# Query scores of an agent attention: copied out of PSUM by ScalarE, maximum taken from SBUF, subtraction on GpSimd

## The chip, the cores and the metric

One core of one Trainium2 chip runs the whole program. The metric is the device time of one execution in microseconds (us). PE is TensorE, DVE is VectorE, ACT is ScalarE, POOL is GpSimd, SP is SyncE, which issues the transfers. PEld are PE's weight loads.

## The reference

Four batches (B = 4) of N = 12480 tokens with C = 128 channels and 49 agents, then a feed-forward layer with d_ff = 2048 on all 49920 tokens.

```python
def sm(a, b):
    s = scale * (a @ b.transpose(0, 2, 1))
    s = s - s.max(-1, keepdims=True)
    e = np.exp(s)
    return e / (e.sum(-1, keepdims=True) + 1e-09)
a2k = sm(agents, k)
agent_v = a2k @ v
q2a = sm(q, agents)
x = q2a @ agent_v
h = x @ w_in
out = (h * np.cos(h)) @ w_out
```

What the change touches is the `s - s.max` of `q2a`: for each token, 49 scores against the agents, less their maximum.

## The kernel before

Tokens are taken in groups of 960 (8 tiles of 120 tokens); a batch has 13 groups, the run 52. A group is one unit of query work (its scores, exponentials, weights, and the transposed weights `pT`) and one unit of feed-forward work.

The **main loop** (L545 to L582) has 832 steps, 16 for each group: two chunks of 480 tokens by eight pairs of d_ff blocks. A step multiplies the query weights with the folded matrix `a` into one of three two-bank PSUM buffers `ph` (PE, L553, two matmuls), takes a cosine of it on ACT into `c` (L556), and combines both on DVE into `r` (L558), which frees the `ph` buffer. Four steps later PE multiplies `r` with `w_out` into an accumulator (L575) that ACT copies out after eight steps (L577, `osb`). So `ph` goes round a ring: PE, ACT, DVE, PE, with three buffers.

Everything else is laid between those steps by a hand-written plan (L450 to L541): the query scores and key scores of later groups, the exponentials in a few bursts, the agents' values, and the folding of the next batch's matrix. A **query** (L336) loads 960 tokens, multiplies their eight tiles with the agents into one PSUM bank (L90, 16 PE records), takes the maxima on DVE (L345) and subtracts them on DVE into a slice of the SBUF tile `e` (L352). The bank comes from a pool of two (`small()`), of which the accumulator `po` holds one nearly always; the other serves queries, key scores, transposes and value sums in turn, and the next user's matmuls wait until the last reader is done. Three queries (`wide=True`, before the main loop) use a `ph` buffer instead; 49 use `small()`. The maxima go to `mx2`, a tile with two buffers.

Several queries form a **piece**, and a **burst** takes one exponential of a whole piece (L356), after which DVE sums it (L360) and takes reciprocals. The exponential needs another ACT table than the cosine, so a burst is a table load, the exponentials of the key scores (L216) and of the piece, and a table load back. In each of the batches after the first there are three bursts; at the first of them three queries of a later piece are laid right beside it (`beside`, L482 to L486, L519). Key scores (L156) are copied out of PSUM by ACT (L173) and DVE takes a running maximum of the copy (L184); beside the very first burst of the main loop three of them are copied by DVE instead (`by_vector`, L490).

POOL multiplies `e` with the reciprocals (L366, 10 steps before the group's first step), PE transposes (L375, from 7 steps before it), ACT copies (L377), POOL makes `pT` of it (L380, L381, four instructions). POOL also subtracts the key maxima (L212, three long instructions for a batch) and adds up the key exponentials (L224).

The order on each engine is laid down when the program is built: the framework places an instruction once its inputs are ready by its own estimate of the times, and of those ready the one that comes first in the program. It is pinned to program order only for the exponentials and the first loads (`keep_in_program_order`). An engine then works through its own list, and an instruction that waits holds up those behind it.

Of the kernel before, what the change touches and what calls it, by code (L numbers as in the profile page):

```python
# [9 lines left out]
F32 = mybir.dt.float32  # L10
# [5 lines left out]
AX = mybir.AxisListType  # L16
# [3 lines left out]
TT = 120  # L20
GT = 8
HT = GT // 2
# [18 lines left out]
def agent_attention_cos_ffn(ctx, tc, qT, kT, v, agT, w_in, w_out, outT):  # L41
    nc = tc.nc
    NB, _, N = qT.shape
    NA = agT.shape[2]
# [39 lines left out]
    def scores(sb, src, b, ps):  # L84

        xt = sb.tile([P, GRP], F32, name="xt", bufs=3)
        load(xt, src)
        ps = ps[:TT, :GT * NA].rearrange("p (t a) -> p t a", a=NA)
        for t in range(GT):
            nc.tensor.matmul(ps[:, t, :], xt[:, t * TT:(t + 1) * TT], ag[:, b, :], start=True, stop=True)  # L90
        return ps

    def scores_twice(xt, src, b, ps):

        load(xt, src)
        ps = ps[:TT, :, :HT * 2 * NA].rearrange("p h (t x a) -> p h t x a", x=2, a=NA)
        for t in range(GT):
            nc.tensor.matmul(ps[:, t // HT, t % HT], xt[:, t * TT:(t + 1) * TT], twice(ag[:, b, :]),  # L98
                             start=True, stop=True)
        return ps[:, :, :, 0, :]  # L100
# [201 lines left out]
    with ExitStack() as pools:  # L302
        sb = pools.enter_context(tc.tile_pool(name="sb", bufs=2))
# [3 lines left out]
        def small():  # L307
            return ps_1.tile([P, 512], F32, name="one")

        def pair():  # L310
            return ps_h.tile([P, 2, 512], F32, name="ph")
# [4 lines left out]
        a = [sb.tile([KR, DFF], F32R, name=f"a{i}", bufs=1) for i in range(2)]  # L316
# [16 lines left out]
        e_of, rz_of = {}, {}  # L333
        PIECES = 5

        def query(n, piece, wide=False):  # L336
            b, g = n // NG, n % NG
            src = qT[b, :, g * GRP:(g + 1) * GRP]
            if wide:
                ps = scores_twice(sb.tile([P, GRP], F32, name="xt", bufs=3), src, b, pair())  # L340
            else:
                ps = scores(sb, src, b, small()).rearrange("p (h t) a -> p h t a", h=2)
            mx = sb.tile([TT, GT], F32, name="mx2")
            mx = mx.rearrange("p (h t) -> p h t", h=2)
            nc.vector.reduce_max(mx, ps, axis=AX.X)  # L345
            if n == piece[0]:
                e = sb.tile([TT, PIECES * GT, NA], F32, name="e", bufs=4)
                rz = sb.tile([TT, PIECES * GT], F32, name="rz2", bufs=4)
                for i, k in enumerate(piece):
                    e_of[k], rz_of[k] = e[:, i * GT:(i + 1) * GT], rz[:, i * GT:(i + 1) * GT]  # L350
                    e_of[piece], rz_of[piece] = e[:, :len(piece) * GT], rz[:, :len(piece) * GT]
            nc.vector.tensor_sub(e_of[n].rearrange("p (h t) a -> p h t a", h=2), ps,  # L352
                                 mx.unsqueeze(3).to_broadcast([TT, 2, HT, NA]))

        def query_exp(piece):
            tc.keep_in_program_order(nc.scalar.activation(e_of[piece], e_of[piece], AF.Exp, scale=SC))  # L356
# [53 lines left out]
        for n in first:  # L410
            pre(NG, query, n, first, True)
# [41 lines left out]
        def extra(n, f, *args, dense=False):  # L453


            while n in taken or (n - LAG) % NP not in ((1, 2, 3, 4, 5) if dense else (1, 3, 5)):
                n += 1
            taken.add(n)
            plan(n, f, *args)
            return n  # L460
# [5 lines left out]
        def spread_out(todo, t, end):  # L466

            for i, lot in enumerate(todo):
                t = extra(t, *lot) + 1
                if i + 1 < len(todo):  # L470
                    t += max(0, (end - t) // (len(todo) - i - 1) - 1)
            return t
# [6 lines left out]
        def scored(piece):  # L479
            return [(query, n, piece) for n in piece]  # L480
# [7 lines left out]
        t = spread_out(scored(early), 0, 0) + 2  # L488
# [3 lines left out]
        for b in range(1, NB):  # L492
            o, ps = (b - 1) * PER, pieces[b - 1]
# [7 lines left out]
            t = spread_out(both, t, o + BURSTS[0] - 14)  # L501
            plan(t, ab[b].top)
            t = extra(t, ab[b].across)
            t = extra(t + 1, ab[b].spread)
# [4 lines left out]
            for k, at in enumerate(BURSTS):  # L509
# [7 lines left out]
                t = at + 6  # L517
# [4 lines left out]
                else:  # L522
                    todo = []
                    for g in range(lots[2][0], NG):
                        plan(t, ab[b].add, g)
                        t = extra(t, ab[b].values, g) + 2
                t = spread_out(todo, t, o + BURSTS[min(k + 1, 2)] - 4)
            plan(t, ab[b].total)
            t = extra(t + 1, ab[b].inverse) + 1
            i = b % 2  # L530
            for c in range(DFF // 512):
                t = extra(t, ab[b].project, c, a[i]) + 1
            t = extra(t, ab[b].project_out, wio, b1[i], b2[i])
# [3 lines left out]
        for piece in pieces[NB - 1]:  # L537
            at = (NB - 1) * PER + BURSTS[0]
            t = spread_out(scored(piece), t, at - 6)
# [5 lines left out]
        for n in range(NSTEP + LAG):  # L545
            pinned[0] = n < NP
            if n < NSTEP:
# [6 lines left out]
                h = ph[:, :, :CH]  # L554
# [42 lines left out]
    with tc.If(far):  # L597
        with ExitStack() as pools:
            sb = pools.enter_context(tc.tile_pool(name="gsb", bufs=2))
# [8 lines left out]
            p = sb.tile([TT, HT, 2 * HI], F32, name="p", bufs=1)  # L608
# [114 lines left out]
```

## Time and profile before

| | |
|---|---|
| median of 3 runs | 1256.7 us (1256.64 to 1257.83) |
| the profiled execution's own time | 1252.39 us |
| its span, first to last instruction | 1250.6 us |
| mean granted TensorE clock | 0.986 of full speed |
| busy share of the span | PE 94%, DVE 87%, ACT 77%, POOL 25% |
| share of the chain that ended last | PE 68%, DVE 14%, ACT 11%, issue 4%, DMA 2% |

Busy shares are means over stages. PE's records overlap one another, so its 94% is not 94% of its work. The chain follows the last instruction back, at each step to what released it or to the instruction before it on its engine, so that a wait which nothing else covers shows up in it. Until 120 us the kernel sets up the first batch and starts the main loop; the stages of batches two to four follow, about 300 us each (from 120, 420 and 720 us); after about 960 us only the last batch's own groups are left.

### The profile page before, as it was taken

To read this page: it belongs to the slowest core of one execution; us is meant where nothing else is said; L and a number is where in the kernel's file an instruction comes from. 1 tells how busy PE (TensorE), PEld (TensorE's weight loads), DVE (VectorE), ACT (ScalarE), POOL (GpSimd) and SP (SyncE) were. 2 spreads that over 40 slices of the span, in tenths; PEclk is the share of its full clock that TensorE was granted. 3 is DMA by queue.
4 is the path that set the end of the run, shared out by engine and by line. 5 is a ranking of instruction groups with operands and counts; after the bars stand their busy time and mean duration, and the time that the engine had idled before them with its cause. 6 is when DMAs were issued, how large, how long until landed. Compare 5 with 4: busy or idle time off the path is not lost.

```text
span 1250.6 us, 17276 instructions
## 1 busy us (share of the span) xinstructions
PE 1177.9 (94%) x6349; PEld 957.6 (77%) x6349; DVE 1089.8 (87%) x1220; ACT 959.0 (77%) x1127; POOL 314.1 (25%) x340
## 2 busy tenths in 40 slices
PE   7989999899999999989999999998999999998997
PEld 7877877778887887877787887877778776776674
DVE  5888888878889888887889889887888999999997
ACT  2357777777778777777878777777887888889996
POOL 1301212512321212162332212115331322113220
PEclk9989999999999999989999999998999999999999
DMA  8963232224422232322241232322321001000000
GB/s 307 246 185 111 80 110 68 76 77 127 126 65 79 79 98 77 95 79 83 73 130 50 78 110 65 97 93 79 96 80 48 32 32 48 17 32 17 32 32 35
DMA packets 39190, 107.74 MB, mean 86 GB/s; under 512 B 4345, under 2 KB 4729, under 8 KB 39097
## 3 DMA queue, kind: packets, MB, share of 16 engines
q1 hardware_dynamic: 39096, 106.55, 27.0%
q8 instruction: 52, 0.85, 0.3%
q14 instruction: 42, 0.34, 0.1%
HBM read 80.97 MB, written 25.56 MB: 85 GB/s over the span
## 4 chain that ended last, share of the span: by engine, by line
PE 68%; DVE 14%; ACT 11%; issue 4%; DMA 2%; POOL 0%; SPq 0%; ACTq 0%; DVEq 0%
PE ph L553 25%; PE one L575 18%; PE one L90 12%; DVE r L558 11%; ACT c L556 6%; PE one L235 5%; ACT osb L577 3%; PE one L375 2%; PE ph L98 2%; PE one L571 2%; PE one L572 2%; DVE mx L345 1%; DMA raw<-w_out 1%; DMA xt<-kT 1%; PE one L266 1%
## 5 line engine op out<-in xcount | busy, mean ns | idle before, releaser
L558 DVE SCALAR_TENSOR_TENSOR r<-c,ph 128x960 fp32r<-128x960 f32 x832 | 924.9, 1149 | 91.1 <-ACT c L556 83.1
L556 ACT ACTIVATE c<-ph 128x960 f32<-128x960 f32 x832 | 794.2, 977 | 220.5 <-PE ph L553 200.9
L553 PE MATMUL ph<-pT,a 113*128 113x480 f32 x1664 | 544.2, 408 | 26.7 <-DVE r L558 24.3
L575 PE MATMUL one<-r,w 128*128 128x480 f32 x1664 | 518.2, 391 | 3.9 <-ACT osb L577 3.5
L553 PEld LDWEIGHTS ph<-pT,a 113*128 113x128 f32 x1664 | 285.7, 191 | 138.8 <-DVE r L558 63.5
L575 PEld LDWEIGHTS one<-r,w 128*128 128x128 f32 x1664 | 311.1, 191 | 52.4 <-ACT osb L577 6.9
L90 PEld LDWEIGHTS one<-ag,xt 128*120 128x120 f32 x1408 | 175.5, 189 | 42.7 <-ACT osb L577 24.4
L366 POOL TENSOR_TENSOR p<-e,rz 120x392 f32<-120x392 f32 x52 | 47.5, 917 | 574.2 <-PE one L375 468.5
L90 PE MATMUL one<-ag,xt 128*120 128x49 f32 x1408 | 174.8, 268 | 16.8 <-issue 8.6
L381 POOL TENSOR_TENSOR pT<-p,pT 49x480 fp32r<-49x480 f32 x104 | 126.1, 1212 | 8.0
L380 POOL CAST pT<-p 49x480 fp32r<-49x480 f32 x104 | 60.5, 582 | 153.0 <-ACT p L377 149.9
L235 PEld LDWEIGHTS one<-s,vt 120*128 120x128 f32 x624 | 77.3, 191 | 10.0 <-DVE av L240 3.6
L235 PE MATMUL one<-s,vt 120*128 120x98 f32 x624 | 79.0, 273 | 2.5 <-DVE av L240 1.4
L577 ACT COPY osb<-one 128x480 f32<-128x480 f32 x104 | 57.7, 554 | 2.9 <-PE one L575 2.9
L224 POOL TENSOR_TENSOR es<-es,s 120x392 f32<-120x392 f32 x36 | 36.7, 1019 | 59.1 <-ACT s L216 56.7
L345 DVE TENSOR_REDUCE mx<-one 120x8 f32<-120x392 f32 x49 | 27.5, 561 | 17.8 <-PE one L90 17.8
L212 POOL TENSOR_TENSOR s<-s,mxb 120x1568 f32<-120x1568 f32 (+1 forms) x9 | 31.6, 3544 | 44.8 <-DVE mxb L208 44.8
L571 PE MATMUL one<-pT,b 113*128 113x480 f32 x104 | 40.2, 387 | 0.0
L572 PE MATMUL one<-pT,b 113*128 113x480 f32 x104 | 40.1, 385 | 0.0
L375 PEld LDWEIGHTS one<-ident,p 120*113 120x113 f32 x208 | 29.2, 177 | 13.6 <-ACT osb L577 9.1
L375 PE MATMUL one<-ident,p 120*113 120x120 f32 x208 | 34.1, 275 | 2.7 <-ACT osb L577 2.7
L377 ACT COPY p<-one 113x480 f32<-113x480 f32 x52 | 29.0, 558 | 6.4 <-PE one L375 5.9
(91 smaller groups left out, 503.2 us busy)
## 6 DMA issues: line engine op xcount, KB each, us to landing
xt<-qT SPq DMA_DIRECT2D x52, 480.0 KB, 3.5
vt<-v SPq DMA_DIRECT2D x104, 240.0 KB, 3.4
outT<-osb SPq DMA_DIRECT2D x51, 480.0 KB, 2.6
xt<-kT SPq DMA_DIRECT2D x46, 480.0 KB, 3.5
c<-kT SPq DMA_DIRECT2D x6, 480.0 KB, 5.7
raw<-w_in SPq DMA_DIRECT2D x8, 256.0 KB, 5.1
raw<-w_out SPq DMA_DIRECT2D x8, 256.0 KB, 6.6
outT<-osb SPq DMA_DIRECT2D x2, 240.0 KB, 2.8
```

The lines of the kernel that those rows point to most:

```text
L90: nc.tensor.matmul(ps[:, t, :], xt[:, t * TT:(t + 1) * TT], ag[:, b, :], start=True, stop=True)
L235: nc.tensor.matmul(po, vt[:, t, :], twice(e[:, t, :]), start=(t == 0 and (g == 0 or not lone)), stop=(t == GT - 1 and (g == NG - 1 or not ...
L375: nc.tensor.transpose(pt[:KR, t * TT:(t + 1) * TT], p_in[n % 2][:, t, :KR], ident[:TT, :TT])
L380: nc.gpsimd.tensor_copy(pT[own, c], p[own])
L381: nc.gpsimd.tensor_sub(pT[other, c], p[own], pT[own, c].bitcast(F32))
L553: nc.tensor.matmul(ph[:, j, :CH], ai[:, f], pTs[q % 3][:, c], start=True, stop=True)
L556: nc.scalar.activation(cos, h, AF.Sin, bias=HALF_PI, scale=1.0)
L558: nc.vector.scalar_tensor_tensor(r, cos, 1.0, h, op0=ALU.subtract, op1=ALU.mult)
L571: nc.tensor.matmul(po, b1[k], pTs[q % 3][:, c], start=False, stop=False)
L572: nc.tensor.matmul(po, b2[k], pTs[q % 3][:, c], start=False, stop=False)
L575: nc.tensor.matmul(po, w1[:, f, :], r[:, j, :], start=(f == 0), stop=(f == NF - 1))
L577: nc.scalar.copy(osb[:, c * CH:(c + 1) * CH], po)
```

## The change

The 49 queries on `small()` are changed. ACT copies the scores from the PSUM bank into their slice of `e`; DVE takes the maxima from `e` in SBUF; POOL subtracts them in place in `e`. The three wide queries keep both operations on DVE and on PSUM. The tiles `e` and `rz2` are now allocated ahead of `mx2`. Nothing is pinned, and no transfer, matmul or exponential is added or moved.

```diff
             else:
                 ps = scores(sb, src, b, small()).rearrange("p (h t) a -> p h t a", h=2)
-            mx = sb.tile([TT, GT], F32, name="mx2")
-            mx = mx.rearrange("p (h t) -> p h t", h=2)
-            nc.vector.reduce_max(mx, ps, axis=AX.X)
             if n == piece[0]:
                 e = sb.tile([TT, PIECES * GT, NA], F32, name="e", bufs=4)
...
-            nc.vector.tensor_sub(e_of[n].rearrange("p (h t) a -> p h t a", h=2), ps,
-                                 mx.unsqueeze(3).to_broadcast([TT, 2, HT, NA]))
+            e = e_of[n].rearrange("p (h t) a -> p h t a", h=2)
+            if not wide:
+                nc.scalar.copy(e, ps)
+                ps = e
+            mx = sb.tile([TT, GT], F32, name="mx2")
+            mx = mx.rearrange("p (h t) -> p h t", h=2)
+            nc.vector.reduce_max(mx, ps, axis=AX.X)
+            on = nc.vector if wide else nc.gpsimd
+            on.tensor_sub(e, ps, mx.unsqueeze(3).to_broadcast([TT, 2, HT, NA]))
```

## Rows read from the trace of the kernel before

**Rows 1.** The chain that ended last, whole run, share of the span by line

```profile
by line: PE ph L553 24.9%; PE one L575 17.9%; PE one L90 11.9%; DVE r L558 10.9%; ACT c L556 6.0%; PE one L235 5.0%; issue 3.9%; ACT osb L577 3.3%; PE one L375 1.8%; PE ph L98 1.7%; PE one L571 1.7%; PE one L572 1.6%; DVE mx L345 1.3%; DMA 
```

**Rows 2.** The same chain in a steady stretch, 420 to 480 us

```profile
by line: PE ph L553 27.3%; PE one L90 23.2%; PE one L575 19.1%; DVE r L558 11.1%; ACT osb L577 5.6%; ACT c L556 4.9%; DVE mx L345 2.4%; PE one L375 2.1%; PE one L571 1.9%; PE one L572 1.8%; issue 1.0%
```

**Rows 3.** Busy time, 420 to 480 us: PE, PEld, DVE, ACT, POOL; then line 173 alone

```profile
420.00:480.00 60.00, 57.38 (x324) 47.57 (x323) 53.00 (x55) 46.61 (x58) 13.11 (x15) 1.00 0.27 84
...
420.00:480.00 60.00, 2.42 (x5) 1.00 0.27 84
```

**Rows 4.** Chain pieces around one steady query: start us, us, what

```profile
447.28 1.16 DVE r L558
448.43 0.47 DVE mx L345
448.91 1.07 DVE r L558
...
450.02 0.70 PE ph L553 x2
```

**Rows 5.** Timeline of the same query: start us, us, engine, line, [idle before it <-releaser]

```profile
446.27 2.73 ACT L556 ACTIVATE c<-ph 128x960 f32<-128x960 f32 x3 [1.18 <-PE ph L553]
...
450.02 0.70 PE L553 MATMUL ph<-pT,a 113*128 113x480 f32 x2 [0.33 <-DVE r L558]
...
450.36 5.61 DVE L558 SCALAR_TENSOR_TENSOR r<-c,ph 128x960 fp32r<-128x960 f32 x5
```

**Rows 6.** Waits of the whole run: us in total, times, longest us

```profile
DVE mx L345 <- PE one L90: 17.8, 12, 2.7
...
PE one L90 <- issue: 8.6, 3, 2.9
```

**Rows 7.** Timeline of one of five queries that follow each other closely

```profile
300.49 0.57 DVE L345 TENSOR_REDUCE mx<-one 120x8 f32<-120x392 f32 x1 [1.10 <-PE one L90]
...
301.42 0.97 ACT L556 ACTIVATE c<-ph 128x960 f32<-128x960 f32 x1 [1.81 <-PE ph L553]
...
302.26 0.67 PE L553 MATMUL ph<-pT,a 113*128 113x480 f32 x2 [0.22 <-DVE r L558]
```

**Rows 8.** Timeline of the first burst with queries beside it

```profile
241.04 1.49 ACT L356 ACTIVATE e<-e 120x1568 f32<-120x1568 f32 x1
...
243.84 2.70 ACT L556 ACTIVATE c<-ph 128x960 f32<-128x960 f32 x3
...
245.46 0.56 DVE L352 TENSOR_TENSOR e<-one,mx 120x392 f32<-120x392 f32 x1
...
246.12 2.82 PE L90 MATMUL one<-ag,xt 128*120 128x49 f32 x16 [2.87 <-issue]
```

**Rows 9.** Busy time right after it (engines as in Rows 3), granted TensorE clock 0.56

```profile
246.00:253.00 7.00, 6.88 (x27) 6.21 (x28) 6.31 (x10) 2.48 (x3) 4.93 (x6) 0.56 0.27 78
```

**Rows 10.** Groups by line and shape: times, busy us, mean ns, idle before, releaser

```profile
L352 DVE TENSOR_TENSOR e<-one,mx 120x392 f32<-120x392 f32 x49 | 27.4, 560 | 0.2
...
L173 ACT COPY s<-one 120x392 f32<-120x392 f32 x36 | 17.4, 484 | 5.7 <-PE one L90 5.4
...
L360 DVE TENSOR_REDUCE rz<-e 120x8 f32<-120x392 f32 x1 | 0.6, 551 | 0.0
```

**Rows 11.** A subtraction as a piece of the chain

```profile
835.14 0.48 DVE e L352
```

**Rows 12.** GpSimd's multiplication of the same shape: ns minimum, median, maximum

```profile
L366 POOL TENSOR_TENSOR p<-e,rz x52: 838/846/3740, 45.9 to 1176.3; 120x392 f32<-120x392 f32 x52
```

**Rows 13.** Shortest way from a last subtraction to the piece's exponential

```profile
109.75 0.56 DVE L352 TENSOR_TENSOR e<-one,mx 120x392 f32<-120x392 f32 x1
...
112.98 1.85 ACT L356 ACTIVATE e<-e 120x1960 f32<-120x1960 f32 x1
```

**Rows 14.** A long stretch of GpSimd reading SBUF, and DVE beside it

```profile
231.27 5.59 DVE L558 SCALAR_TENSOR_TENSOR r<-c,ph 128x960 fp32r<-128x960 f32 x5
...
231.49 10.53 POOL L212 TENSOR_TENSOR s<-s,mxb 120x1568 f32<-120x1568 f32 x3 [14.80 <-DVE mxb L208]
```

## The prediction, made before the changed kernel was run

> **What bounds the kernel now.** I read the chain that ended last first, whole and then in a steady stretch. PE's four main lines hold most of it, and what PE waits for shows as DVE r 10.9%, ACT c 6.0%, ACT osb 3.3% and DVE mx 1.3% [rows 1]. 1.3% of 1250.6 us is 16.3 us: that is what the maxima (L345) cost on the path. In the steady stretch mx has 2.4% of 60 us, three pieces of 0.48, one for each query there, and the list adds up to 100%, so neither the key scores' copy on ACT (L173) nor their running maximum on DVE (L184) is on the chain there, though five copies ran [rows 2, 3]. Then the busy times of that stretch: DVE 53.0 of 60 us (88%), ACT 46.6 (78%), POOL 13.1 (22%) [rows 3]. PE's 57.4 overstates it: a pair of L553 that takes 0.70 after a wait stands at some 0.44 in the chain where pairs follow each other. So DVE is the engine with least to spare, and the loss is latency: PE waits for a `ph` buffer that r frees late.
>
> How a query makes r late is in its own rows. In the steady case mx stands between two r's; the second ends 0.48 later, and PE, which has already sat 0.33 us, starts the next pair right on its end [rows 4, 5]. In the close case mx heads DVE's list before its scores exist: DVE sits 1.10 us, the r behind it has had its input all along (ACT idle for 1.81), and PE waits 0.22 for that r [rows 7]. DVE waited for scores like this twelve times, 17.8 us in all [rows 6]. Three of these, of 2.7 us, stand in bursts; nine of about 1.08 are close cases (17.8 - 8.1 = 9.7).
>
> **The change, part by part.** The sum goes against the profiled execution, 1252.4 us with 1250.6 of span; the median of the runs is 1256.7, 4.3 above it, and I add the same 4.3 at the end.
>
> *The subtraction leaves DVE:* 49 x 0.560 = 27.4 us of work [rows 10]. On the chain it shows only five times, 0.48 to 0.54 each (one of them: [rows 11]), so 2.4 us. Ends: 0, and all 27.4 if every r behind a subtraction is on the path. I take 2.4, since the chain is the nearer row; after the steady subtraction five r's do run back to back, but PE has other work there [rows 5].
>
> *The maximum stays on DVE.* Reading SBUF it costs what it did: 0.551 us for the same shape [rows 10]. But it now comes after a copy, so its place changes. In the nine close cases it can no longer stand ahead of an r that is ready; PE gets back its 0.22 us and the slow restart after it, 0.67 against 0.44 for a pair: 0.45 x 9 = 4.0. Ends: 0, and 9 x 1.1 = 9.9 if all of DVE's wait comes back. In the steady cases the chain has 16.3 less twelve pieces of 0.57 = 9.5 us, about twenty pieces. Either mx still falls between two r's (0) or it falls ahead of or behind the pair that matters (9.5). The row does not decide: it is the framework's order. I take half, 4.7.
>
> *The copy on ACT:* 49 x 0.484 = 23.7 us, from the key scores' copy of the same shape [rows 10]. What hides it is ACT's idle time while PE works through the scores, 1.18 us in the steady case and 1.81 in the close one [rows 5, 7]. Without that cover each copy puts the c behind it, and its r, 0.4 to 0.48 us late. Lower end 0: the key copies are absent from the steady chain [rows 2]. Upper end: as often as the accumulator's copy, 3.3% or 41 us for 104 copies [rows 1], 0.40 each, 19.5 for 49. The key copy is the same shape and place, so near the lower end: I take a tenth of the upper, 2.0 lost.
>
> *The subtraction on POOL:* nearest the multiplication of the same shape with the same kind of broadcast, 0.846 [rows 12]; ends 0.838 and 3.74, its slowest. In all 49 x 0.85 = 41 us on an engine 25% busy. Cover: nothing needs the result until the piece's exponential. A query takes copy 0.48 + max 0.55 + subtraction 0.85 = 1.9 us instead of 1.1, and the shortest way from the end of a last subtraction to its exponential is 112.98 - 110.31 = 2.7 us [rows 13], so the 0.8 fits. If POOL is behind one of its long instructions (10.5 us for three [rows 14]) the exponential waits, and ACT's cosines behind it. These come ahead of the first burst of a batch, whose own piece was finished before; I take 0, at most one such instruction, 3.5 us, for three batches. There is a new wait on DVE too: `mx2` has two buffers, which POOL now frees, so the third of three quick queries waits for POOL with r's behind it. That can happen only at the same three bursts; 0 to 2.4 us each, taken as 0.
>
> *The PSUM bank* is freed by the copy, not by the subtraction. It matters at those three bursts: PE's third block of scores waits until DVE's subtraction at 245.46 ends, 2.87 us [rows 8], three times 8.6 us in all [rows 6]. After the wait the granted clock is 0.56 for 7 us [rows 9], near the lower of the two levels (1.2 of 2.4 GHz); 7 x 0.44 = 3.1 us more. So a burst holds about 6 us that hang on when a bank comes free, 18 us in all. With the change ACT must free it, and ACT has the exponentials until 242.53, a table load, and three cosines from 243.84 to 246.54 [rows 8]. A copy just before those cosines frees the bank 1.7 us sooner, one behind them 1.0 us later. I take 0 and keep both ends as rivals.
>
> No transfer is added; SP's loads wait for the same matmuls as before. The three wide queries keep their operations.
>
> **Sum:** 2.4 + 4.0 + 4.7 - 2.0 = 9.1 us gained; 1252.4 - 9.1 = 1243.3, and with the 4.3 **1247.6 us**.
>
> **A rule weighed against the trace.** While POOL ran 10.5 us of subtractions that read SBUF, five r's beside them took 5.59 us [rows 14]; without POOL, 5.61 [rows 5]. r is not slowed. The Trainium skill, "Perfetto Trace Analysis", section "Optimizing Scalar/DVE Operations", says that offloading to GPSIMD may make sense if DVE is saturated, but that the two share an SBUF read port, so that moving work between them might not help. For r the trace does not bear the second half out. By the rule, each subtraction would hold up one r by its own 0.85 us, and I keep it as the last rival.
>
> **The rivals.**
> *Bursts close too.* The copies fall before the cosines at the three bursts, the 2.87 us gaps shrink by 1.7 and the clock stays up: 3 x (1.7 + 3.1) = 14.4 beyond the forecast, **1233 us**. For it: the gap's end is a DVE instruction queued behind a 1.8 us sum, and the copy needs neither. Against: ACT is full there.
> *No difference.* mx keeps its place between the r's and only the subtraction's 2.4 us come back, or the steady gain is eaten in the bursts: **1254 to 1258 us**. For it: the same rule of order as before places mx.
> *Slower.* At the three bursts ACT's list has both exponentials ahead of the first query's copy. Its bank comes free at 243.0 instead of 240.6, so the second block of scores starts about 1.5 us late; its copy stands behind the three cosines, so the third block starts at about 247.5 instead of 246.1; with the clock low for a further 2 us that is 1.5 + 1.4 + 0.9 = 3.8 a burst, 11.4 in all. If mx also keeps its place, only the 2.4 come back: +9, **1266 us**. It decides as soon as a copy stands behind both the exponentials and the cosines. For it: exponentials are pinned ahead, and key copies beside the very first burst were given to DVE. Against: PE has idle time there anyway.
> *The shared port.* 49 x 0.85 = 41 us if every subtraction stalls an r on the path: up to 1247.6 + 41 = **1289 us**. Against it: the row above.
>
> **How the numbers follow.** Forecast 0.42, bursts close too 0.18, no difference 0.17, slower 0.19, port 0.04. A measurement tells about 0.2% (2.5 us) from no change. Forecast (1241 to 1254) and bursts lie on the faster side; of "no difference" 0.03 is faster, 0.12 same, 0.02 slower; the last two are slower: faster 0.63, same 0.12, slower 0.25. The range goes from 1232, just below the centre of the lowest rival (a third of it left out, 0.06), to 1265, about the centre of the slower one (half left out, 0.09), and leaves out the port: 0.19. The forecast alone has 1241 to 1254: the steady term at 9.5 or 0, the copy at 0 or 4.
>
> **What would show it.** Right: DVE about 27 us less busy, ACT 24 and POOL some 41 more; mx nearly gone as something that waits for PE; mx on the chain at most half of 16 us; no copy of scores among the large lines of the chain. The subtraction on POOL at 0.85. At 238 to 253 us PE's gap about as long as before, with the clock falling after it. Wrong: copies between PE and c on the chain, c waiting behind a copy that itself waits for PE; DVE's maximum waiting for POOL; a longer gap in the three bursts, or none; r longer than 1.15 us beside POOL.

## The result and the profile after

The changed kernel took 1242.4 us (median of four runs, 1237.0 to 1246.1) against 1256.7 for the kernel before: a ratio of 0.989 with an interval of 0.985 to 0.993. Run again (an experiment below) it took 1239.1 against 1256.6, ratio 0.990 (0.987 to 0.993). So 1247.6 was 5 us too slow, inside the range; the gain was 14 to 17 us where the sum had 9.1. The profiled execution was 1242.7 us with 1241.0 of span; that of the second time was 1237.0 with 1235.2.

The changed kernel's page begins with the span and each engine's busy time, share and instructions:

```profile
span 1241.0 us, 17334 instructions
...
PE 1180.0 (95%) x6349; PEld 975.0 (79%) x6349; DVE 1067.3 (86%) x1171; ACT 982.4 (79%) x1176; POOL 353.5 (28%) x389
```

Before, DVE had 1089.8, ACT 959.0 and POOL 314.1: work has moved as the diff says. The changed kernel's groups by line and shape, which answer to [rows 10] (line numbers have shifted by 4; the copy is L351, the maximum L355, the subtraction L357), show what each instruction costs:

```profile
L562 DVE SCALAR_TENSOR_TENSOR r<-c,ph 128x960 fp32r<-128x960 f32 x832 | 924.1, 1149 | 96.2 <-ACT c L560 90.4
...
L357 POOL TENSOR_TENSOR e<-e,mx 120x392 f32<-120x392 f32 x49 | 41.3, 844 | 155.7 <-DVE mx L355 150.9 <-ACT osb L581 3.5
L355 DVE TENSOR_REDUCE mx<-e 120x8 f32<-120x392 f32 x49 | 27.2, 555 | 8.2 <-ACT e L351 8.2
L351 ACT COPY e<-one 120x392 f32<-120x392 f32 x49 | 23.8, 487 | 18.7 <-PE one L90 18.4
```

The prices are those of the sum: 0.844 against 0.85, 0.555 against 0.551, 0.487 against 0.484. r has 1149 ns, as before.

The waits of the whole run (us in total, times, longest) say where DVE mattered less. First the changed kernel, then the one before:

```profile
PE ph L557 <- DVE r L562: 14.2, 39, 4.3
...
PE one L90 <- ACT e L351: 10.9, 3, 3.6
...
DVE mx L355 <- ACT e L351: 8.2, 7, 1.7
```

```profile
PE ph L553 <- DVE r L558: 24.3, 74, 4.3
```

TensorE waited for r 39 times and not 74, 10 us less. In place of the three waits for DVE's subtraction [rows 6] there are three for ACT's copy, a little longer, and at another block of scores (see the bursts below). Nothing on DVE waits for POOL. In the chain of the whole run the maxima (mx) have 10.5 us where they had 16.6; "at most half" was named as a sign of being right, and it did not come.

The steady stretch, 411 to 471 us, has the same shape as [rows 2, 4]. The chain by line, some of its pieces, and the timeline of the same query:

```profile
by line: PE ph L557 27.8%; PE one L90 24.2%; PE one L579 21.4%; DVE r L562 11.1%; ACT c L560 4.9%; ACT osb L581 4.7%; DVE mx L355 2.4%; PE one L576 1.8%; PE one L575 1.8%; issue 0.8%
...
425.14 1.15 DVE r L562
426.29 0.47 DVE mx L355
426.76 1.07 DVE r L562
...
427.88 0.70 PE ph L557 x2
```

```profile
423.19 0.49 ACT L351 COPY e<-one 120x392 f32<-120x392 f32 x1 [0.23 <-PE one L90]
...
424.38 0.47 PE L379 MATMUL one<-ident,p 120*113 120x120 f32 x3
...
426.21 0.55 DVE L355 TENSOR_REDUCE mx<-e 120x8 f32<-120x392 f32 x1
...
426.68 5.42 DVE L562 SCALAR_TENSOR_TENSOR r<-c,ph 128x960 fp32r<-128x960 f32 x5
...
428.11 0.85 POOL L357 TENSOR_TENSOR e<-e,mx 120x392 f32<-120x392 f32 x1
```

Before, the transposes for the next weights, which use the same bank, came only after the subtraction:

```profile
450.78 0.57 PE L375 MATMUL one<-ident,p 120*113 120x120 f32 x4
```

The maximum still stands between two r's with its 2.4%, and TensorE still takes its next pair behind the second r. But the copy lets the transposes (424.38) start ahead of the maximum, where they stood behind the subtraction, and the stretch got shorter. Where, the copy-outs of the output rows (osb) tell: there are 104 at fixed places in the work, and the differences of their start times cut a run into stretches that can be laid beside each other. **Start** is up to the 1st; **first burst** from the 1st to the 5th; **three bursts** the sum of 13th to 15th, 39th to 41st and 65th to 67th; **rest** all else up to the 103rd; **four steady** queries lie between the 27th and the 35th, **two close** ones between the 35th and the 39th (both are part of the rest). All in us, one profiled run each:

| run | start | first burst | three bursts | rest | four steady | two close |
|---|---|---|---|---|---|---|
| before | 97.3 | 48.9 | 91.9 | 998.3 | 89.10 | 46.27 |
| changed | 95.5 | 54.1 | 94.3 | 982.7 | 87.44 | 44.55 |
| changed, again | 91.0 | 51.5 | 94.8 | 983.4 | 87.44 | 44.57 |
| subtraction on VectorE | 92.3 | 48.0 | 96.0 | 992.6 | 88.99 | 45.00 |
| copy on VectorE | 102.9 | 51.0 | 86.5 | 991.3 | 88.35 | 45.35 |
| only beside the bursts | 97.8 | 51.3 | 97.0 | 999.1 | 89.07 | 46.29 |
| beside old | 92.7 | 53.0 | 91.3 | 981.9 | 87.45 | 44.56 |
| beside by VectorE | 97.1 | 54.0 | 85.4 | 982.1 | 87.44 | 44.56 |
| first burst later | 93.1 | 50.7 | 94.5 | 983.3 | 87.44 | 44.56 |
| beside and 3 to 7 by VectorE, later | 103.4 | 50.8 | 84.8 | 982.8 | 87.44 | 44.57 |
| beside by VectorE, later | 91.3 | 49.2 | 84.4 | 982.8 | 87.45 | 44.55 |
| query 3 old | 104.8 | 52.7 | 94.7 | 983.5 | 87.44 | 44.57 |
| no maximum, no subtraction | 95.8 | 52.7 | 97.6 | 971.6 | 86.13 | 43.91 |
| no subtraction | 97.1 | 53.1 | 93.4 | 983.0 | 87.44 | 44.56 |

The change gains some 15 us in the rest, 0.41 for a steady query and 0.86 for a close one, and gives back 2.4 to 2.9 in the three bursts and 2.6 to 5.2 in the first. The start varies from run to run for a reason that was not found (last section), and also holds a gain, found below.

### The profile page after: what moved, and what is told of

It reads as the page before. It is cut to its first block, busy times and chain, and to the rows that moved or that the text cites. A ratio compares the mean times of both kernels' runs of the same rounds, so it can differ in the third digit from the quotient of the medians.

```text
span 1241.0 us, 17334 instructions
## 1 busy us (share of the span) xinstructions
PE 1180.0 (95%) x6349; PEld 975.0 (79%) x6349; DVE 1067.3 (86%) x1171; ACT 982.4 (79%) x1176; POOL 353.5 (28%) x389
## 3 DMA queue, kind: packets, MB, share of 16 engines
q1 hardware_dynamic: 39096, 106.55, 27.4%
## 4 chain that ended last, share of the span: by engine, by line
PE 70%; DVE 12%; ACT 12%; issue 4%; DMA 0%; POOL 0%; ACTq 0%; SPq 0%; DVEq 0%
PE ph L557 25%; PE one L579 18%; PE one L90 12%; DVE r L562 9%; ACT c L560 6%; PE one L235 5%; ACT osb L581 3%; PE ph L235 3%; PE one L575 2%; PE one L576 2%; PE one L379 1%; PE ph L98 1%; ACT e L360 1%; DVE mx L355 1%; PE one L266 1%
## 5 line engine op out<-in xcount | busy, mean ns | idle before, releaser
L562 DVE SCALAR_TENSOR_TENSOR r<-c,ph 128x960 fp32r<-128x960 f32 x832 | 924.1, 1149 | 96.2 <-ACT c L560 90.4
L90 PEld LDWEIGHTS one<-ag,xt 128*120 128x120 f32 x1408 | 180.6, 194 | 49.5 <-ACT osb L581 27.9
L90 PE MATMUL one<-ag,xt 128*120 128x49 f32 x1408 | 180.2, 273 | 21.5 <-ACT e L351 10.9
L370 POOL TENSOR_TENSOR p<-e,rz 120x392 f32<-120x392 f32 x52 | 44.3, 857 | 474.2 <-PE one L379 397.2
L357 POOL TENSOR_TENSOR e<-e,mx 120x392 f32<-120x392 f32 x49 | 41.3, 844 | 155.7 <-DVE mx L355 150.9
L379 PEld LDWEIGHTS one<-ident,p 120*113 120x113 f32 x208 | 31.7, 178 | 12.2 <-ACT osb L581 7.1
L212 POOL TENSOR_TENSOR s<-s,mxb 120x1568 f32<-120x1568 f32 (+1 forms) x9 | 31.6, 3537 | 29.8 <-DVE mxb L208 29.8
L379 PE MATMUL one<-ident,p 120*113 120x120 f32 x208 | 37.6, 274 | 2.3 <-ACT osb L581 2.3
L351 ACT COPY e<-one 120x392 f32<-120x392 f32 x49 | 23.8, 487 | 18.7 <-PE one L90 18.4
```

The lines of the kernel that those rows point to most:

```text
L379: nc.tensor.transpose(pt[:KR, t * TT:(t + 1) * TT], p_in[n % 2][:, t, :KR], ident[:TT, :TT])
L562: nc.vector.scalar_tensor_tensor(r, cos, 1.0, h, op0=ALU.subtract, op1=ALU.mult)
```

## The experiments

Each kernel is the changed one with the edit shown, beside runs of the kernel before on the same chip; ratios are against those. The edits are shown by what they do. In the kernels that ran, `query` has an argument `by` through which they are made: "act" the changed path, "old" that of before, "dve" the changed path with VectorE's copy.

**Which of the two gains: the subtraction or the copy?** The subtraction goes back to VectorE, the copy stays.

```diff
-            on = nc.vector if wide else nc.gpsimd
+            on = nc.vector
```

> Copy on ACT, maximum from SBUF on DVE, and the subtraction on DVE too (from SBUF), so GpSimd does nothing new. Theory (the steady gain is the 0.56 us of subtraction that DVE no longer does): three steady groups go back from 65.6 us (changed kernel) to 66.4 to 66.8 (66.8 before), and the run to 1250 to 1258 us. Rival (the gain comes from the copy: the PSUM bank is free sooner and DVE's maximum no longer heads its list while the scores are missing): three groups stay at 65.4 to 65.8 us and the run at 1239 to 1246.

1248.9 us, ratio 0.994 (0.991 to 0.997), just under what the theory named. The steady gain is gone (three queries 66.7), most of the close queries' gain stays (45.00 of 46.27 against 44.55), and of the 15 us of the rest 5.7 stay. So the larger part, 9.6 us, goes when the subtraction is back on VectorE. TensorE's waits for r are 52 here, 39 in the changed kernel and 74 before: 13 of the 35 that went are the subtraction's. The steady stretch shows it on the chain; first its list by line, then pieces of it:

```profile
by line: PE ph L563 26.0%; PE one L90 19.1%; PE one L585 19.0%; DVE r L568 18.4%; ACT c L566 6.5%; DVE e L361 3.1%; ACT osb L587 2.8%; DVE mx L359 2.4%; PE one L581 1.1%; PE one L582 1.1%; issue 0.8%
...
443.96 0.47 DVE mx L359
444.44 1.06 DVE r L568
445.50 0.62 DVE e L361
446.12 1.07 DVE r L568
```

Here maximum and subtraction both delay r's that TensorE wants. The subtraction is longer than before, 646 ns in the mean over 49 where it had 560 [rows 10]. Reading SBUF is not enough to make it so: the 22 subtractions with no instruction of GpSimd beside them take 558 ns in the mean, the 26 that have one beside them for over half of their length 715. One of each, the first with GpSimd's cast beside it:

```profile
444.48 1.22 POOL L388 CAST pT<-p 49x480 fp32r<-49x480 f32 x2
445.42 0.71 DVE L361 TENSOR_TENSOR e<-e,mx 120x392 f32<-120x392 f32 x1
...
512.15 0.56 DVE L361 TENSOR_TENSOR e<-e,mx 120x392 f32<-120x392 f32 x1
```

GpSimd's own busy time is 321.2 us here and 314.1 before, for the same work. So a VectorE instruction with both inputs in SBUF and GpSimd's work do slow each other in this kernel, and 9.6 us is what 31.6 us of subtraction cost on VectorE, a little more than the old 27.4 would.

**Is it ScalarE's copy, or a copy at all?** VectorE copies, GpSimd subtracts: VectorE's load is that of before, 1088.1 us busy.

```diff
-                nc.scalar.copy(e, ps)
+                nc.vector.tensor_copy(e, ps)
```

> The copy out of PSUM on DVE instead of ACT, maximum on DVE from SBUF, subtraction on GpSimd: DVE does two instructions per query as before, ACT none, GpSimd one. Theory (DVE relief): three steady groups at 66.4 to 66.9 us; what is left of the gain is in the close queries and the bursts, run 1246 to 1256. Rival (bank free sooner): DVE frees the bank 0.56 us after its scores, sooner than before, so the run stays at 1237 to 1245.

1238.8 us, ratio 0.986 (0.983 to 0.990): as fast as the changed kernel though VectorE is as busy as before. The time is the rival's, but the rest does not say what the rival said: it gains 7.0 (0.19 a steady query, 0.46 a close one), less than the change; the bursts get 5.3 us shorter where the change makes them longer. So the path with a copy is worth 6 to 7 us in the rest, whichever engine makes the copy (that the bank comes free earlier is the likely reason; no run shows it alone); taking 0.56 us off VectorE is worth another 8.3 (991.3 against 983.0); and in the bursts ScalarE is the wrong engine.

**The bursts alone.** The changed path only for queries 3 to 7 and beside the bursts; then the reverse, the old path beside the bursts; then the copy there on VectorE.

```diff
-        def query(n, piece, wide=False):
+        def query(n, piece, wide=False, by="old"):
...
             for lot in todo[:3]:
+                if lot[0] is query:
+                    lot += (False, "act")
                 extra(at, *lot, dense=True)
```

> The changed path only for the nine queries laid beside a batch's first burst and for the five early queries; all others as before. Theory (there the change loses: ACT holds the bank behind the exponentials, PE's gap in the three bursts grows from 2.9 to 3.6 us and the clock stays low for longer, and the first burst of the main loop loses up to 4.6): 1257 to 1264 us. Rival (these losses are chance, of one trace): 1252 to 1257.

1256.7 us, ratio 1.001 (0.999 to 1.004). By its time this is the rival's, just under what the theory named; the trace has the losses that the theory named, with the three bursts together 5.1 us longer and the first 2.4. That the run is not longer for it fits the gain of the start (below), but was not taken apart. The rest is within 0.9 of before, so the new order in which the tiles are allocated does nothing by itself.

```diff
+                if lot[0] is query:
+                    lot += (False, "old")
```

> The changed kernel with the query groups beside the bursts back on the path of before; all others, queries 3 to 7 too, as changed. Theory: those groups alone make the bursts longer (+0.4 to +1.7 us each in the changed kernel against before), since ScalarE's copy stands behind the exponentials there; then the three bursts are within 0.4 us of before (30.77, 30.44, 30.65) and the run is 1 to 3 us under the changed kernel, 1236 to 1238. Rival: the bursts are longer because of what steady queries do before them; then they stay at +0.4 to +1.7 and the run at 1239.

1235.3 us, ratio 0.985 (0.981 to 0.988). The bursts are at 30.39, 30.43 and 30.53 us, all within 0.4 of before, and the time is just under what was named. The loss there is those groups' copies, not what steady queries leave behind.

```diff
+                if lot[0] is query:
+                    lot += (False, "dve")
```

> The changed kernel, but the nine queries beside the three first bursts are copied out of PSUM by DVE, which has nothing to do while ACT takes exponentials. Theory (the gap of 3.6 us hangs on ACT freeing the bank): the gap falls below 2 us, the granted clock stays above 0.8 there, and the run gains 3 x 2 to 6 us: 1226 to 1237. Rival (PE has nothing else to do in a burst whatever frees the bank): 1240 to 1246.

1233.2 us, ratio 0.980 (0.976 to 0.983); the bursts are 6.4 us shorter than before and 8.8 shorter than with the change. How ScalarE's copy loses is in the timelines of the burst that [rows 8] show. Before, the second of the three blocks of scores ran beside the exponentials, since VectorE had freed the bank; the third waited 2.87 us [rows 8]:

```profile
241.47 1.78 PE L90 MATMUL one<-ag,xt 128*120 128x49 f32 x16
```

Then the changed kernel, with the windows behind it (columns as in [rows 3]; the last three are granted clock, DMA share, GB/s):

```profile
240.77 1.52 ACT L216 ACTIVATE s<-s 120x1568 f32<-120x1568 f32 x1
242.19 1.50 ACT L360 ACTIVATE e<-e 120x1568 f32<-120x1568 f32 x1
...
245.00 0.97 ACT L560 ACTIVATE c<-ph 128x960 f32<-128x960 f32 x1
245.87 0.48 ACT L351 COPY e<-one 120x392 f32<-120x392 f32 x1
...
246.40 3.44 PE L90 MATMUL one<-ag,xt 128*120 128x49 f32 x16 [3.62 <-ACT e L351]
```

```profile
246.00:256.00 10.00, 9.60 (x40) 8.94 (x41) 6.14 (x9) 5.00 (x7) 8.46 (x10) 0.50 0.29 71
```

The copy of the first query's scores stands behind both exponentials, a table load and one cosine, so that already TensorE's second block waits 3.62 us for it; the other two bursts have the same wait, 3.62 and 3.61. The granted clock behind it is 0.50 for the whole 10 us, its lower level (1.2 GHz), where [rows 9] had 0.56 for 7. With VectorE's copies in the same burst, the second block and the third:

```profile
243.96 1.78 PE L90 MATMUL one<-ag,xt 128*120 128x49 f32 x16
...
246.40 1.88 PE L90 MATMUL one<-ag,xt 128*120 128x49 f32 x16 [0.38 <-DVE e L355]
...
250.38 1.14 PE L563 MATMUL ph<-pT,a 113*128 113x480 f32 x2 [2.10 <-DVE r L568]
```

```profile
246.00:256.00 10.00, 7.52 (x31) 6.31 (x31) 9.68 (x12) 5.60 (x7) 9.70 (x11) 0.68 0.34 99
```

The second block runs beside the exponentials again, and the third starts after 0.38 us. A wait of 2.10 for r comes 4 us later, and the clock still falls, but for less of the stretch: 0.68, where the theory named over 0.8.

**Is the maximum still paid for?** The small query groups' maximum and subtraction are left out, and the exponential is taken of the bare scores; then the subtraction alone.

```diff
-            nc.vector.reduce_max(mx, ps, axis=AX.X)
-            on = nc.vector if wide else nc.gpsimd
-            on.tensor_sub(e, ps, mx.unsqueeze(3).to_broadcast([TT, 2, HT, NA]))
+            if wide:
+                nc.vector.reduce_max(mx, ps, axis=AX.X)
+                nc.vector.tensor_sub(e, ps, mx.unsqueeze(3).to_broadcast([TT, 2, HT, NA]))
```

> The changed kernel without the maximum and without the subtraction of the small query groups (ScalarE's copy stays; the exponential is taken of the bare scores). Theory one: in the steady stretches it is VectorE's time that counts, whatever the instruction is, since the maximum stands between two r; 0.56 us of subtraction gave back 0.41 us a query there, so 0.555 us of maximum give back about as much again: four steady queries (87.4 us in the changed kernel, 89.1 before) at 85.7 to 86.2, and the run at 1226 to 1233 us. Rival: with the subtraction gone TensorE alone sets the pace, and the maximum is hidden: four steady queries at 87.2 to 87.5, the run at 1240 to 1243. The bursts gain nothing by either (+0.5 to +1.2 us each against before), since ScalarE's copy frees the bank there.

1231.6 us, ratio 0.983 (0.979 to 0.987). Four steady queries come down to 86.13 and the rest by another 11 us, to 971.6. The steady chain and the wait for r:

```profile
by line: PE ph L563 36.2%; PE one L585 30.8%; PE one L90 23.6%; ACT osb L587 2.8%; PE one L582 2.2%; PE one L581 2.2%; PE one L383 2.1%; issue 0.4%
```

```profile
PE ph L563 <- DVE r L568: 11.1, 29, 4.5
```

VectorE is off the steady chain altogether. The bursts lose more than in the changed kernel, 5.8 us against before; why was not followed up.

```diff
-            on = nc.vector if wide else nc.gpsimd
-            on.tensor_sub(e, ps, mx.unsqueeze(3).to_broadcast([TT, 2, HT, NA]))
+            if wide:
+                nc.vector.tensor_sub(e, ps, mx.unsqueeze(3).to_broadcast([TT, 2, HT, NA]))
```

> The changed kernel without the subtraction of the small query groups; ScalarE's copy and VectorE's maximum stay (the exponential is taken of the bare scores). Theory: GpSimd's 0.844 us lie in slack of several microseconds ahead of the exponentials, so that nothing changes: four steady queries at 87.3 to 87.5 us and the run at 1237 to 1241. Rival: the end of the subtraction on GpSimd sets when the exponentials or GpSimd's later weights and halves come; then four steady queries fall below 87.0 and the run below 1236. With the run without maximum and subtraction (86.13 and 1231.6) this tells which of the two those gains came from.

1242.2 us, ratio 0.989 (0.985 to 0.993); four steady queries at 87.44, to the hundredth as in the changed kernel. The median lies 1.2 us over what the theory named, with a start of 97.1; the stretches it spoke of did not move. GpSimd's subtraction is free, and the 11 us are the maximum's.

**The start.** One query of 52, number 3, goes back to the old path; and the changed kernel is run again.

```diff
-        t = spread_out(scored(early), 0, 0) + 2
+        t = spread_out([lot + (False, "old" if lot[1] == 3 else "act") for lot in scored(early)], 0, 0) + 2
```

> The changed kernel with one query of 52, number 3, back on the path of before (maximum and subtraction on VectorE, straight from the bank). Theory: in the kernel before these two stand ahead of the first r on VectorE, TensorE waits 2.2 us at 82 us of the run and is at half clock for the some 5 us behind it, and the change takes that wait away; so here the wait is back, the first copy-out of an output row block is 5 to 6 us later than in the changed kernel (96 to 98 us where the start ran at full clock, 100 to 103 where it did not), and the run is at 1243 to 1247 us against 1239.1 for the changed kernel on the same chip. Rival: the start varies by itself (91 to 97 us over the profiles of the changed path); then the first copy-out is at 91 to 97 us and the run at 1238 to 1241.

> The changed kernel once more, with its switch for the three engines built in but set as the change has it: 1240 to 1245 us; it gives the changed kernel more runs on the chip of the other three, to compare them with.

With query 3 old: 1246.3 us, ratio 0.994 (0.992 to 0.997), 12 runs; the changed kernel again: 1239.1, 11 runs. One query is worth some 5 to 7 us here. The reason is in the kernel before, outside the rows that I had read (the windows' columns as above):

```profile
79.56 0.57 DVE L345 TENSOR_REDUCE mx<-one 120x8 f32<-120x392 f32 x1 [0.94 <-PE one L90]
...
80.16 0.57 DVE L352 TENSOR_TENSOR e<-one,mx 120x392 f32<-120x392 f32 x1
...
82.19 0.67 PE L553 MATMUL ph<-pT,a 113*128 113x480 f32 x2 [2.17 <-DVE r L558]
```

```profile
83.00:88.00 5.00, 5.00 (x22) 4.70 (x21) 3.40 (x4) 1.89 (x2) 0.00 (x0) 0.50 0.06 14
```

The same place in the changed kernel, in the second profile:

```profile
78.65 0.49 ACT L352 COPY e<-one 120x392 f32<-120x392 f32 x1
...
78.89 0.70 PE L563 MATMUL ph<-pT,a 113*128 113x480 f32 x2 [0.27 <-DVE r L568]
```

```profile
80.00:85.00 5.00, 5.00 (x38) 4.44 (x37) 4.69 (x6) 3.37 (x6) 0.84 (x1) 1.00 0.68 220
```

Before, VectorE waits 0.94 us for the scores, takes maximum and subtraction ahead of the first r's, TensorE waits 2.17 us, and the clock behind it is 0.50. With the copy on ScalarE the r's come first and the clock stays at 1.00. From the end of TensorE's last work ahead of that wait to the first copy-out it is 17.3 us before (80.02 to 97.30) and 12.4 in the changed kernel (78.62 to 91.03): **4.9 us**. With query 3 old the wait is back:

```profile
89.66 0.67 PE L563 MATMUL ph<-pT,a 113*128 113x480 f32 x2 [2.17 <-DVE r L568]
```

It ends 15.1 us ahead of the copy-out, as before (12.1 in the changed kernel). The first copy-out at 104.8 is later than I had named, because the clock had been low from 40 to 70 us as well.

**The first burst.** It begins two steps later, so that its exponentials fall behind a copy-out.

```diff
-        t = spread_out(scored(early), 0, 0) + 2
+        t = spread_out(scored(early), 0, 0) + 4
```

> The changed kernel, with the exponentials of the first burst (queries 3 to 7) two steps later, so that they fall behind the copy-out of an output row block and not ahead of it. Theory: the 4.6 us that the changed kernel loses between its first and third copy-out (32.1 us against 27.5) come from the copy-out that stands behind the exponentials on ScalarE and holds a bank; then this stretch is 27 to 29 us here, the gap of 3.2 us on TensorE ahead of L90 is gone, and the run is at 1236 to 1240 us against 1242.4 for the changed kernel. Rival: the loss has nothing to do with that order (it is the clock in the start of the run, or the copies of queries 3 to 7); then the stretch stays at 31 to 33 us and the run at 1241 to 1244.

1237.4 us, ratio 0.988 (0.984 to 0.992). The first line is the changed kernel, the second this one:

```profile
112.85 3.44 PE L90 MATMUL one<-ag,xt 128*120 128x49 f32 x16 [3.20 <-ACT osb L581]
```

```profile
113.24 2.77 PE L90 MATMUL one<-ag,xt 128*120 128x49 f32 x16 [1.11 <-DVE s L171]
```

The wait for ScalarE's copy-out is gone, but 1.11 us for VectorE's copy of key scores take its place, and the clock falls all the same. The stretch from the 1st to the 3rd copy-out is 29.2 us, just above what the theory named; the same changed kernel had 32.1 in one profile and 29.5 in another, and the ratios overlap.

One more run has the other order. With the subtraction on VectorE the copy-out happened to be placed ahead of the exponential (the windows' columns as above):

```profile
103.86 0.56 ACT L587 COPY osb<-one 128x480 f32<-128x480 f32 x1
...
105.73 1.84 ACT L364 ACTIVATE e<-e 120x1960 f32<-120x1960 f32 x1
```

```profile
104.00:124.00 20.00, 19.62 (x126) 16.46 (x126) 18.57 (x22) 16.31 (x18) 5.62 (x6) 1.00 0.40 124
```

All of ScalarE's copies are in it, TensorE has no such wait, the clock stays at 1.00, and the first burst takes 48.0 us, 48.9 before. All runs with the exponential ahead of the copy-out have the wait (3.18 to 3.55 us) and 51.3 us or more. So ScalarE's copies as such do not lengthen the first burst, and every run with the exponential first does lose; with the order turned round a run can still lose to another wait, as the one above did (50.7). How the loss divides between the wait and the clock stays open.

**The versions put together.** First with VectorE's copies beside the bursts and for queries 3 to 7 (`by="dve"` in both places) and the later burst; then the same with ScalarE's copies for queries 3 to 7.

> Three edits on the changed kernel: the copies of the query groups beside the bursts and of queries 3 to 7 are done by VectorE, and the first burst is two steps later. Theory: the gains add up, 1233.2 (the copies beside bursts on VectorE) less some 3 to 4 for the first burst: 1228 to 1231 us. Rival, the first burst's loss was not its order: 1232 to 1236 us.

1232.3 us, ratio 0.983 (0.980 to 0.987): 1.3 us over the theory and where the rival had it, but for another reason. The bursts are short (84.8), but the start is 103.4, as with all copies on VectorE (102.9): there VectorE's copy of query 3 takes the place that the maximum had, and TensorE waits again. (In both profiles the clock was low from 40 to 60 us as well; with that and ScalarE's copies the start is 95.5 and 97.1.)

```profile
87.03 1.14 PE L563 MATMUL ph<-pT,a 113*128 113x480 f32 x2 [1.91 <-DVE r L568]
```

> Two edits on the changed kernel: the copies beside the bursts are VectorE's, and the first burst is two steps later; queries 3 to 7 keep ScalarE's copy. Theory: the copies of queries 3 to 7 on VectorE cost the start 5 us (first copy-out at 103 us against 97) in the run that had those two edits as well, so that this one has its first copy-out at 92 to 97 us, the bursts at 27.9 to 28.8 and the run at 1227 to 1230. Rival: the two edits don't add up with the start (the wait at 85 us comes back, or the first burst stays as long): 1231 to 1234.

**1225.0 us, ratio 0.978 (0.974 to 0.983)**, the fastest, 2 us under what the theory named; its first copy-out is at 91.3 and its bursts at 27.8, 27.9 and 28.7. It beats the kernel before by 2.2% and the changed one (0.990, 0.987 to 0.993), whose interval lies above its own. Over the version without the later burst (0.980, 0.976 to 0.983) the intervals overlap: the shift's own part is not settled, though the first burst went from 54.0 to 49.2 between these two profiles.

## Why the prediction was right, and where it was not

The direction, the range and the prices of the single instructions held. That the total came out near was in part luck: terms that were too small and terms that were missing offset each other.

- **The subtraction leaves VectorE, "so 2.4 us" (step that failed: a term mis-sized).** It was priced by its five pieces on the chain. The runs put it at 8.3 us (against VectorE's copy) to 9.6 (against VectorE's subtraction, which is longer there): 0.17 to 0.20 us each over 49, a third of its duration. The upper end, 27.4, was about three times too large. The same was found for the maximum, whose 27.2 us of work cost 11 still. So in this kernel 0.56 us of VectorE's time in a query costs, in the mean over 49, a third of it or a little more on the way to the end, whether the chain before the change names the instruction or not. "PE has other work there" was argued from one stretch of five r's; a steady query gains 0.23 us (against VectorE's copy) to 0.39 (against VectorE's subtraction) when the subtraction goes, and 13 of PE's waits for r go with it.
- **The maximum's place and ScalarE's copy, 4.0 + 4.7 - 2.0 = 6.7.** As a sum it came near, by luck: the changed path with the subtraction on VectorE gains 5.7 in the rest, and the path with VectorE's copy 7.0. The close queries gave more than the 0.45 each that was said: 1.27 of their 1.72 us for two, 0.64 each, are there with the subtraction still on VectorE. The steady half failed: mx keeps its place there and its 2.4% of the chain, and four steady queries gain 0.12 us with the subtraction still on VectorE (0.70 and not 0.56 us each there, which may hide some), 0.76 with VectorE's copy. How much of the copy's 2.0 was really lost was not measured by itself.
- **The copy's cover.** The copy waits for TensorE 30 times, 18.4 us, and in the steady query above it ends before the next cosine's input is there. It is not among the large lines of the chain.
- **GpSimd's subtraction, 0.** Shown: leaving it out leaves the steady queries at 87.44 and the rest at 983.0. VectorE did not wait for it either.
- **The bursts, 0.** Wrong by 2.4 to 2.9 us for three. In kind it is the "slower" rival: a copy stands behind exponentials and a cosine, and the clock is low for longer. But the copy behind the cosine is the first query's, which the rival had right behind the exponentials, and it holds up the second block of scores by 3.62 us; the rival had 1.5 there, and the third block held up behind three cosines. The loss is 0.4 to 1.7 us a burst and not the rival's 3.8; why so little of the longer wait is left at the end was not measured by itself. The rival's other half, that only the subtraction's 2.4 us come back, did not come. Beside old and beside by VectorE show that these groups alone do it.
- **The first burst and the start (steps missing).** The sum had only the three later bursts. The first loses 2.6 to 5.2 us where the exponential stands ahead of the copy-out, a wait of 3.20 us with a low clock behind it; in the one run with ScalarE's copies that has neither this wait nor another it takes 48.0 us, and nothing is lost. The start gains 4.9, shown by query 3. I read the chain in steady stretches and one burst, and never the first queries, where one wait of 2.17 us drew half clock behind it.
- **The sum, remade:** -15 (rest) + 2.7 (bursts) + 2.6 to 5.2 (first burst) - 4.9 (start) = -12 to -15 us, against medians 14.3 and 17.5 apart; the start's own spread is larger than the difference. The two profiles with the clock at 1.00 from 40 to 60 us, before and changed again, are 15.4 us apart.
- **The rivals.** "Bursts close too" needs the copies ahead of the cosines; the first fell behind one. "No difference" is out by the rest. "The shared port" is out for r, which reads one input from SBUF and one from PSUM: it has 1149 ns over 832 in both kernels. It is not out for an instruction with both inputs in SBUF: VectorE's subtraction from SBUF took 715 ns in the mean beside GpSimd and 558 without. The Trainium skill, "Perfetto Trace Analysis", section "Optimizing Scalar/DVE Operations", says that moving work between DVE and GPSIMD might not help because of a shared SBUF read port. By that rule the move could have brought nothing; here it was worth 8 to 10 us.

## What to carry to other kernels

The chain shows one path; an engine at 87% that feeds the bound one costs time with every instruction in its queue, so price what leaves it by all its instructions times a share, not by its pieces on the chain. The share (here a third, in the mean) has to be measured; taking one such instruction out, as was done with the maximum, gives it. When a bank must come free, choose the engine by what else stands in its queue at that place: here ScalarE in steady queries and at the start, VectorE beside exponentials. Read the waits of the bound engine from the very first one, and count what the clock does behind each.

## What was not expected of the hardware

The times of one kernel come in two sorts. The 11 runs of the changed kernel fall into 1236.9 to 1239.1 and 1243.2 to 1246.7 us, the 16 of the kernel before beside them into 1247.5 to 1252.1 and 1256.5 to 1262.1. The profiles show a place in the start where such a difference can come from; the stretch from 40 to 60 us in the first and in the second profile of the changed kernel:

```profile
40.00:60.00 20.00, 20.00 (x110) 20.00 (x108) 12.00 (x24) 5.07 (x10) 4.15 (x6) 0.57 0.68 195
```

```profile
40.00:60.00 20.00, 18.93 (x165) 18.39 (x164) 16.30 (x32) 8.57 (x15) 9.11 (x7) 1.00 0.92 241
```

The granted clock is 0.57 in one and 1.00 in the other, with 110 matmuls done against 165. The two kernels run the same instructions in the same order on every engine, TensorE had waited 1.44 us for ScalarE just ahead of it in both, and the kernel before shows 1.00 there. What decides it was not found, and that it is what parts the two sorts is not shown. It is why no difference of a few us is read from a single time here, and why the stretches are compared.
